# The tail of a decode block: w4 in five pieces instead of eight, the projection's row copied into spare bytes of w4's buffer, eight narrow last rows instead of six

## The chip, the cores and the metric

The kernel runs on one core of a Trainium2 chip. The metric is the device time of one execution in microseconds (us). Every run also has a span, from the first to the last profiled instruction of the core; the time is longer than the span by what lies outside it. Ratios are computed as the mean time of one kernel's runs over that of the other's of the same rounds, so they are not quite the ratio of the medians.

## The reference

One token goes through two branches that share the normalised input, and everything is summed. Cut to what matters:

```python
def reference(A_x, A_k_cache, A_v_cache, A_wq, A_wo, B_x, B_w1, B_w2, B_w3, B_w4):
    # A: 32 query heads, 4 key/value heads, 65536 cached keys of 128
    q = (x @ wq) ...                                   # 1024 -> 32 x 128
    p = softmax(q . k * 128 ** -0.5)
    o = p . v                                          # [cut]
    a = o @ wo                                         # 4096 -> 1024
    # B: a gated MLP for one position (w1, w2 act on a zero-padded shift), then
    h2 = gelu(layernorm(x1) @ w3) @ w4                 # 1024 -> 3584 -> 1024
    return x + a + (x1 + h2)
# bf16 data; caches 4 x 65536 x 128 each for k and v; w4 is 3584 x 1024
```

## The kernel before

One queue loads everything in a fixed order into three buffers of 64 KB a partition: wq, w3, w1 and w2, then the key and value blocks of 8 MB in turn, with wo before the last value block, and w4 last. A buffer is refilled when its last reader is done. What the change touches is the end of that stream. All products of one token are accumulated in one PSUM bank, psB (PSUM is where TensorE's sums stand until another engine copies them out): `row_acc(j, ...)` puts the j-th half of the output row into column group j of TensorE, so two matmuls run side by side. The last rows of w4 ("narrow") run as four quarters in four column groups in another pair of banks, into which the sum of everything else is added by a small fp32 matmul.

```python
W4_PIECES = (6, 5, 6, 4, 3, 2, 1, 1)     # rows (of 2 KB a partition) of each load of w4, 28 in all
NARROW = 6                               # last rows in four column groups
AHEAD = 3                                # of these, the ones before the sums
# [cut]
    def project(g):                      # o of head group g times its part of wo, 16 matmuls
        # [cut] groups 0..2 into tail["rows"][0:1, 0:2, :], group 3 by row_acc

    def add_projection():
        rows = ppool.tile([1, 2, 512], F32, name="o_rows", tag="p")   # tag "p": one buffer, shared with p_sb
        nc.vector.tensor_copy(out=rows[:], in_=tail["rows"][0:1, 0:2, :])
        for j in range(2):
            row_acc(j, ident_f[0:1, 0:1], rows[0:1, j, :])

    def compute_w4(lo, hi):              # row c of w4: two matmuls of 512 columns
        wt = st.tiles["w4"]
        for c in range(lo, hi):
            for j in range(2):
                row_acc(j, hT[:, c:c + 1], wt[:, D * c + 512 * j:D * c + 512 * (j + 1)])
# [cut]
    for g in range(HKV - 1):
        project(g)
    add_projection()
    compute_v(NU - 1)                    # last value block, its scaling, its gather (pe) and oT
    early = sum(W4_PIECES[:2])
    compute_w4(0, early)
    project(HKV - 1)
    compute_w4(early, FC - NARROW)
    sums = ogpool.tile([64, 512], F32, name="sums", tag="og")
    nc.scalar.copy(out=sums[:], in_=psB[0:64, :])
    # [cut] quarters: two PSUM banks; quarter_acc: four matmuls of 256 columns, one a column group
    narrow_rows(FC - NARROW, FC - NARROW + AHEAD, start=True)
    quarter_acc(...)                     # adds the sums, fp32
    narrow_rows(FC - NARROW + AHEAD, FC)
    # [cut] two casts, one store
```

`p_sb`, the probabilities, is read by the last value matmul. So the copy into `o_rows`, which shares its buffer, has to wait for it.

## Time and profile before

| | before |
|---|---|
| time, median of the first three runs | 401.93 us (400.98 to 401.99) |
| span of the profile | 399.0 us |
| loaded | 169.87 MB, 98.9% of the 16 load engines' time |
| TensorE busy, VectorE busy | 59%, 52% |

In the lines below PE is TensorE's matmuls, PEld its weight loads, DVE is VectorE, ACT ScalarE, POOL GpSimd, and an L with a number is a line of the kernel. "Half rate" means that the trace lists TensorE's granted clock as 0.50 of full. These are lines of the page of before: busy time of the engines, the busy share of the load engines in 40 slices, the packets, and the queues (q1 carries the loads, q8 fetches instructions).

```profile
span 399.0 us, 2590 instructions
...
PE 234.1 (59%) x1368; PEld 45.6 (11%) x874; DVE 209.4 (52%) x155; ACT 27.6 (7%) x36; POOL 5.3 (1%) x28
...
DMA  9998999999999999999999999999999999999996
...
DMA packets 4576, 170.03 MB, mean 426 GB/s; under 512 B 467, under 2 KB 469, under 8 KB 982
...
q1 hardware_dynamic: 4560, 169.87, 98.9%
q8 instruction: 9, 0.15, 0.2%
```

The load queue is full from end to end. The time is the time of 170 MB of loads, plus a start and a tail. The tail is read from the timeline (start, duration, engine, line, operation; in brackets the idle time ahead of it and what ended it):

```profile
384.41 1.21 DVE L459 COPY o_rows<-o_acc 1x1024 f32<-1x1024 f32 x1 [14.25 <-PE oacc L414]
...
385.68 1.05 PE L223 MATMUL psB<-o_rows,ident_f 1*32 1x512 f32 x4 [1.33 <-DVE o_rows L459]
...
388.53 0.80 PE L435 MATMUL pm_e<-ol,sel8big 128*128 128x129 f32 x2
...
392.88 2.11 PE L223 MATMUL psB<-big,hT 128*32 128x512 bf16 x18
...
395.46 0.58 ACT L486 COPY sums<-psB 64x512 f32<-64x512 f32 x1 [27.91 <-PE psB L223]
...
396.09 0.64 PE L493 MATMUL pm_r<-sums,ident_f 64*32 64x256 f32 x8 [0.35 <-ACT sums L486]
...
396.66 0.51 PE L493 MATMUL pm_r<-big,hT 128*32 128x256 bf16 x12
...
397.25 0.43 DVE L510 CAST out_t<-pm_r 64x256 bf16<-64x256 f32 x1 [6.91 <-PE pm_r L493]
```

The copy of the projection's row (L459) stood behind the last value matmul; TensorE then waited 1.33 us for it. The last line of L493 covers the last three rows of w4, twelve matmuls; the last four of them, for the last row, start at 396.89, while the trace has the last piece landed at 396.68. The chain that ended last says the same: it goes through TensorE (psB, pm_r), not through a load.

```profile
384.41 1.22 DVE o_rows L459
...
385.68 2.92 PE psB L223 x14
...
389.33 5.57 PE psB L223 x45
...
395.46 0.59 ACT sums L486
...
396.09 1.13 PE pm_r L493 x20
...
397.25 0.43 DVE out_t L510
```

### The profile page before, as it was taken

The numbers are of one execution on the slowest core, as the hardware profiler recorded it, in microseconds if no ns is written. First come the engines' busy times: TensorE is split into PE (matmuls) and PEld (weight loads), VectorE is DVE, ScalarE is ACT, GpSimd is POOL, SyncE is SP. The second block draws the span as 40 slices with busy tenths as digits, with TensorE's granted clock in tenths as the row PEclk, the third lists the DMA queues.
The fourth block names the chain that finished last, engine by engine and source line by source line (L and its number), as shares of the span: only waits on it lengthen the run. The fifth ranks groups of instructions, "written<-read, shape, count | busy, mean of one in ns | idle before, by whom it ended". The sixth has DMA issues, their size and how long they took to land.

```text
span 399.0 us, 2590 instructions
## 1 busy us (share of the span) xinstructions
PE 234.1 (59%) x1368; PEld 45.6 (11%) x874; DVE 209.4 (52%) x155; ACT 27.6 (7%) x36; POOL 5.3 (1%) x28
## 2 busy tenths in 40 slices
PE   0561960691569237733974296439443945494987
PEld 0210000000200110011001110101010002010133
DVE  0620010965196559634953795269449932884131
ACT  1001010003000200020002000200100020002000
POOL 2000000000000000000000000000000000000000
PEclk9996896696769787966695679569976886598799
DMA  9998999999999999999999999999999999999996
GB/s 421 420 454 372 437 453 473 434 420 420 422 428 420 440 466 435 420 427 427 435 420 440 447 447 420 422 420 447 427 442 440 440 420 394 425 450 447 393 420 255
DMA packets 4576, 170.03 MB, mean 426 GB/s; under 512 B 467, under 2 KB 469, under 8 KB 982
## 3 DMA queue, kind: packets, MB, share of 16 engines
q1 hardware_dynamic: 4560, 169.87, 98.9%
q8 instruction: 9, 0.15, 0.2%
q14 instruction: 1, 0.01, 0.0%
q10 hardware_dynamic: 6, 0.00, 0.0%
HBM read 169.87 MB, written 0.00 MB: 426 GB/s over the span
## 4 chain that ended last, share of the span: by engine, by line
DMA 48%; DVE 25%; PE 21%; ACT 3%; another core or an unknown queue 2%; issue 1%; DVEq 0%; ACTq 0%
DMA big<-in_A_k_cache_dram 42%; DVE big L359 19%; PE sc L364 8%; DMA big<-in_A_wq_dram 5%; PE oacc L414 5%; PE o_acc L453 3%; DVE mx L369 3%; ACT p_sb L382 3%; DVE p_sb L385 2%; PE psB L223 2%; PE psq L289 1%; DVE m L373 0%; PE pm_mx L371 0%; PE pm_mx L378 0%
## 5 line engine op out<-in xcount | busy, mean ns | idle before, releaser
L364 PE MATMUL sc<-big,qdiag 128*128 128x512 bf16 x512 | 130.2, 416 | 64.2 <-DVE big L359 63.9
L359 DVE STREAM_TRANSPOSE big<-big 128x4096 f32<-128x4096 f32 x32 | 139.4, 4413 | 50.7 <-DMA big<-in_A_k_cache_dram 50.7
L414 PE MATMUL oacc<-big,p_sb 128*32 128x512 bf16 x512 | 45.1, 522 | 34.5 <-DVE p_sb L385 34.5
L369 DVE TENSOR_REDUCE mx<-sc 128x1 f32<-128x2048 f32 x8 | 18.3, 2292 | 30.4 <-PE sc L364 30.4
L364 PEld LDWEIGHTS <-qdiag 128*128 128x128 bf16 x128 | 13.2, 103 | 176.7 <-issue 146.4
L382 ACT ACTIVATE p_sb<-sc,nball 128x2048 bf16<-128x2048 f32 x8 | 15.7, 1967 | 218.3 <-DVE nball L380 218.3
L385 DVE STREAM_TRANSPOSE p_sb<-p_sb 128x2048 bf16<-128x2048 bf16 x8 | 18.5, 2312 | 18.0 <-ACT p_sb L382 18.0
L414 PEld LDWEIGHTS <-p_sb 128*32 128x32 bf16 x512 | 16.8, 126 | 59.5 <-DVE p_sb L385 35.1
L289 PE MATMUL psh<-big,ln_rep_b 128*32 128x512 bf16 (+1 forms) x64 | 12.4, 941 | 8.6 <-DMA big<-in_B_w_dram 8.6
L453 PE MATMUL o_acc<-big,oT 128*1 128x512 bf16 x48 | 13.5, 453 | 2.4 <-ACT p_sb L382 2.4
L371 PE MATMUL pm_mx<-ident_f,mx 128*1 128x128 f32 x8 | 2.2, 270 | 19.1 <-DVE mx L369 19.1
L328 DVE STREAM_TRANSPOSE h_row<-h_row 128x896 bf16<-128x896 bf16 x1 | 1.1, 1111 | 21.7 <-ACT h_row L327 21.7
L423 DVE SCALAR_TENSOR_TENSOR og<-oacc,wb,og 128x512 f32<-128x512 f32 x4 | 3.0, 746 | 15.2 <-PE oacc L414 15.2
L459 DVE COPY o_rows<-o_acc 1x1024 f32<-1x1024 f32 x1 | 1.2, 1212 | 14.2 <-PE oacc L414 14.2
L237 PE MATMUL pm_ln<-ln_rowsum_a,ones_f 128*128 128x1 f32 x2 | 0.6, 347 | 12.6 <-DVE ln_rowsum_a L235 12.6
L435 PE MATMUL pm_e<-ol,sel8big 128*128 128x129 f32 x8 | 2.6, 414 | 7.9 <-DVE ol L434 7.9
L313 POOL COPY qdiag<-qx 32x32 bf16<-32x32 bf16 x16 | 3.2, 203 | 279.2 <-PE sc L364 250.5
L228 DVE STREAM_TRANSPOSE x_t<-x_row 32x256 bf16<-32x256 bf16 x4 | 2.5, 616 | 8.2 <-DMA x_row<-in_A_x_dram 8.1
L223 PE MATMUL psB<-big,hT 128*32 128x512 bf16 x44 | 6.5, 448 | 0.0
L289 PE MATMUL psq<-big,ln_rep_a 128*32 128x512 bf16 x64 | 5.2, 499 | 1.1 <-DMA big<-in_A_wq_dram 1.1
L378 PE MATMUL pm_mx<-ident_f,rep 1*128 1x1 f32 x8 | 1.9, 235 | 5.0 <-DVE rep L375 5.0
L420 ACT COPY og<-oacc 128x512 f32<-128x512 f32 x4 | 2.3, 585 | 34.3 <-PE oacc L414 34.3
(101 smaller groups left out, 75.1 us busy)
## 6 DMA issues: line engine op xcount, KB each, us to landing
big<-in_A_wo_dram SPq DMA_DIRECT2D x1, 8192.0 KB, 36.8
big<-in_B_w_dram SPq DMA_DIRECT2D x1, 7168.0 KB, 38.1
big<-in_B_w_dram SPq DMA_DIRECT2D x2, 2048.0 KB, 45.9
big<-in_B_w_dram SPq DMA_DIRECT2D x2, 1536.0 KB, 27.3
big<-in_B_w_dram SPq DMA_DIRECT2D x1, 1280.0 KB, 24.1
big<-in_B_w_dram SPq DMA_DIRECT2D x1, 1024.0 KB
big<-in_B_w_dram SPq DMA_DIRECT2D x1, 768.0 KB, 30.8
big<-in_B_w_dram SPq DMA_DIRECT2D x1, 512.0 KB, 31.6
```

The costliest lines, as they stand in the source:

```text
L223: nc.tensor.matmul(psB[32 * j:32 * j + 32, :], lhsT=lhsT.to_broadcast([lhsT.shape[0], 32]), rhs=rhs, start=start, stop=False, tile_positio ...
L289: nc.tensor.matmul(acc[32 * q:32 * q + 32, i, 0:n], lhsT=rep[:, c, :], rhs=cols(c, i, q), start=(c == 0), stop=(c == DC - 1), tile_positio ...
L313: nc.gpsimd.tensor_copy(out=qdiag[at, LEAD:].rearrange("p (x c) -> p x c", x=4)[:, :, 32 * a:32 * a + 8], in_=qx[at, :, 8 * g:8 * g + 8])
L359: nc.vector.transpose(out=words, in_=words)
L364: nc.tensor.matmul(sc[:, e, :], lhsT=qdiag[:, c0:c0 + P], rhs=cols[:, s, e, :, b2, :, r], start=(s == 0 and b2 == 0 and r == 0), stop=(s = ...
L369: nc.vector.reduce_max(out=mx[:], in_=sc[:].rearrange("p e n -> p (e n)"), axis=AX.X)
L382: nc.scalar.activation(out=p_sb[:], in_=sc[:], func=ACTF.Exp, bias=nball[:, b:b + 1], scale=SCALE, accum_out=group["lall"][:, b:b + 1])
L385: nc.vector.transpose(out=flat, in_=flat)
L414: nc.tensor.matmul(oacc[32 * q:32 * (q + 1), :], lhsT=pT[:, e, 32 * t:32 * (t + 1)], rhs=vt[:, :, e, t, :], start=(e == 0 and t < 4), stop ...
L423: nc.vector.scalar_tensor_tensor(out=og[:], in0=oacc[:], scalar=wb[:, 1:2], in1=og[:], op0=ALU.mult, op1=ALU.add)
L435: nc.tensor.matmul(pe[:, 0:DH + 1], lhsT=sel8big[:], rhs=ol[:], start=True, stop=True)
L453: nc.tensor.matmul(tail["rows"][0:1, h2, :], lhsT=oT[g][:, j:j + 1], rhs=wt[:, g, j, 512 * h2:512 * (h2 + 1)], start=(g == 0 and j == 0), ...
```

## The change

Its intent: make the end of TensorE's work depend on the last load alone. The w4 loads become fewer and are cut so that a piece of 12 rows may come late and the last piece is still one row. The projection's row is copied, as soon as it is summed, into bytes of w4's own buffer that no w4 load writes, so it no longer waits for the probabilities' buffer. Eight rows instead of six go through the narrow path and five of them ahead of the sums, so that the sums are taken two rows earlier. `issue_after` fixes the order of TensorE's instructions without a wait.

```diff
-W4_PIECES = (6, 5, 6, 4, 3, 2, 1, 1)
-NARROW = 6
-AHEAD = 3
+W4_PIECES = (8, 12, 5, 2, 1)
+FIRST = 3
+AT_ONCE = 1
+NARROW = 8
+AHEAD = 5
 # [cut: row_acc, compute_v, group_rows and project return their matmul]
-    def add_projection():
-        rows = ppool.tile([1, 2, 512], F32, name="o_rows", tag="p")
-        nc.vector.tensor_copy(out=rows[:], in_=tail["rows"][0:1, 0:2, :])
+    def copy_projection():
+        tail["o"] = st.tiles["w4"][0:1, FC * D:FC * D + 2 * D].bitcast(F32)
+        nc.vector.tensor_copy(out=tail["o"].rearrange("p (j n) -> p j n", j=2), in_=tail["rows"][0:1, 0:2, :])
+
+    def add_projection():
         for j in range(2):
-            row_acc(j, ident_f[0:1, 0:1], rows[0:1, j, :])
+            row_acc(j, ident_f[0:1, 0:1], tail["o"][:, 512 * j:512 * (j + 1)])
 # [cut]
-    add_projection()
-    compute_v(NU - 1)
-    early = sum(W4_PIECES[:2])
-    compute_w4(0, early)
-    project(HKV - 1)
-    compute_w4(early, FC - NARROW)
+    copy_projection()
+    summed = compute_v(NU - 1)
+    with tc.issue_after(summed):
+        add_projection()
+    early = sum(W4_PIECES[:AT_ONCE])
+    compute_w4(0, FIRST)
+    with tc.issue_after(tail["gathered"]):
+        compute_w4(FIRST, early)
+    projected = project(HKV - 1)
+    with tc.issue_after(projected):
+        compute_w4(early, FC - NARROW)
```

More of the change, by code (lines that the diff above doesn't have):

```diff
@@ L222, in row_acc @@
     def row_acc(j, lhsT, rhs, start=False):
-        nc.tensor.matmul(psB[32 * j:32 * j + 32, :], lhsT=lhsT.to_broadcast([lhsT.shape[0], 32]), rhs=rhs, start=start,
-                         stop=False, tile_position=(0, 32 * j), skip_group_check=True)
+        return nc.tensor.matmul(psB[32 * j:32 * j + 32, :], lhsT=lhsT.to_broadcast([lhsT.shape[0], 32]), rhs=rhs, start=start,
+                                stop=False, tile_position=(0, 32 * j), skip_group_check=True)
     x_t = ppool.tile([P, DC, 32], BF16, name="x_t", tag="p")
@@ L413, in compute_v @@
                 q = t % 4
-                nc.tensor.matmul(oacc[32 * q:32 * (q + 1), :], lhsT=pT[:, e, 32 * t:32 * (t + 1)],
-                                 rhs=vt[:, :, e, t, :], start=(e == 0 and t < 4),
-                                 stop=(e == SUBS - 1 and t >= 12), tile_position=(0, 32 * q))
+                mm = nc.tensor.matmul(oacc[32 * q:32 * (q + 1), :], lhsT=pT[:, e, 32 * t:32 * (t + 1)],
+                                      rhs=vt[:, :, e, t, :], start=(e == 0 and t < 4),
+                                      stop=(e == SUBS - 1 and t >= 12), tile_position=(0, 32 * q))
         st.done(("V", u))
@@ L425, in compute_v @@
         group_rows(g, og, ol)
+        return mm.ins
     oT = {}
@@ L434, in group_rows @@
         nc.vector.tensor_reduce(out=ol[:, 0:DH], in_=og[:].rearrange("p (s d) -> p d s", d=DH), axis=AX.X, op=ALU.add)
-        nc.tensor.matmul(pe[:, 0:DH + 1], lhsT=sel8big[:], rhs=ol[:], start=True, stop=True)
+        tail["gathered"] = nc.tensor.matmul(pe[:, 0:DH + 1], lhsT=sel8big[:], rhs=ol[:], start=True, stop=True).ins
         msk = small.tile([P, 16, 8], F32, name="msk", tag="msk")
@@ L450, in project @@
                 if g == HKV - 1:
-                    row_acc(h2, oT[g][:, j:j + 1], wt[:, g, j, 512 * h2:512 * (h2 + 1)])
+                    mm = row_acc(h2, oT[g][:, j:j + 1], wt[:, g, j, 512 * h2:512 * (h2 + 1)])
                     continue
@@ L455, in project @@
                                  stop=(g == HKV - 2 and j == 7), tile_position=(0, 0))
+        return mm.ins if g == HKV - 1 else None
+    def copy_projection():
+        tail["o"] = st.tiles["w4"][0:1, FC * D:FC * D + 2 * D].bitcast(F32)
+        nc.vector.tensor_copy(out=tail["o"].rearrange("p (j n) -> p j n", j=2), in_=tail["rows"][0:1, 0:2, :])
     def add_projection():
-        rows = ppool.tile([1, 2, 512], F32, name="o_rows", tag="p")
-        nc.vector.tensor_copy(out=rows[:], in_=tail["rows"][0:1, 0:2, :])
         for j in range(2):
-            row_acc(j, ident_f[0:1, 0:1], rows[0:1, j, :])
+            row_acc(j, ident_f[0:1, 0:1], tail["o"][:, 512 * j:512 * (j + 1)])
     def compute_w4(lo, hi):
```

## The prediction

> What bounds the kernel now. The span is 399.0 us; the load queue carries 169.87 MB in packets that fill 98.9% of 16 engines' time (page, part 3), and no slice of DMA is below 8 tenths except the last (part 2). TensorE is busy 59%, VectorE 52%. It is a stream of loads with a tail, and the change touches only the tail, behind the last value block, which lands at 379.27.
>
> The tail, from the timeline and the landings. The 28 rows of w4 follow without a hole: 11 rows have landed at 386.05, 17 at 389.73, 24 at 394.12, 26 at 395.38, 27 at 396.04, all at 396.68: 0.62 us a row, whatever the piece. TensorE runs almost without a hole from 379.9 and is a little late: the wide rows end at 395.4, the copy of the sums takes 0.58, their fp32 matmuls start at 396.09, and only at 396.66 the last three rows go, 0.11 us each. The last row starts at 396.89, 0.2 us after it landed, and ends at 397.17; the casts end at 397.68, the span at 399.0. The chain of waits names TensorE (psB, pm_r) here, but landing and chain end within 0.2 us of each other.
>
> What the change does.
> 1. The projection's row no longer waits for the probabilities' buffer. In before its copy stood behind the last value matmul (VectorE idle 14.2 us, copy 384.41 to 385.62, TensorE idle 1.3 us) and pushed the output scaling back by 1.1 us. After, it is copied near 381, and its fp32 rows follow the value matmuls at about 384.4.
> 2. The gather comes about 1.1 us sooner (near 387.0), the last projection near 389. Holding w4 rows behind the gather can leave TensorE idle 0.9 us; harmless.
> 3. Pieces of 8, 12, 5, 2, 1: estimated landings 384.2, 391.6, 394.7, 396.0, 396.6 (0.62 us a row). The 12-row piece comes late for TensorE, but its 24 matmuls in two column groups take 12 x 0.215 = 2.6 us, to 394.3. The copy of the sums starts there, hidden behind the five narrow rows ahead (5 x 0.11). The sums' matmuls end near 395.8. The last row then waits for its landing alone.
> 4. Three fewer DMAs: a packet of 2 KB takes 0.085 us, one of 4 KB 0.165, so a packet costs some 0.005 us beside its bytes; about 0.1 us of stream in all. Bytes are unchanged.
>
> On the critical path: 0.2 us of TensorE lateness and up to 0.1 us of stream. The 1.3 us hole and VectorE's 1.1 us mostly become slack before the last landing. Gain 0.2 to 0.35 us, under 0.1%, below the run-to-run spread of before (400.98 to 401.99).
>
> Predicted: 401.6 us, 8 in 10 within 400.7 to 402.3. Faster by over 2%: 0.01; within 2%: 0.98; slower: 0.01.
>
> What would show it: last landing within 0.3 us of before; the row's copy before 383; TensorE idle before the last row until its landing; last matmul ending 0.3 us after it instead of 0.5; landing to end of span 2.1 us instead of 2.3.
>
> What would make it wrong: the copy into w4's tile ordered behind w4's loads (then some 10 us lost). TensorE's clock is 0.50 from 387.1 to 390.3 in before; the Trainium skill (TensorE: Matmul & The Clock Gate, Part 1) ties half rate to recent idleness in free-running windows. Half rate over the 24 matmuls at 391.6 would end them near 396.8 and cost up to 2 us.

## The result

| | before | changed |
|---|---|---|
| time, six runs each of the same rounds | 401.26 us median (400.97 to 401.99) | 400.68 us median (400.60 to 400.81) |
| ratio of the runs | | 0.9982 (95%: 0.9969 to 0.9995) |
| span of the profile | 399.0 | 398.7 |
| last w4 landing | 396.68 | 396.50 |

The predicted 401.6 us with its range of 400.7 to 402.3 missed the measured 400.68 us, and the forecast gain of 0.2 to 0.35 us stands against 0.7 us between the means of these runs (0.0018 x 401).

The same lines of the page after the change:

```profile
span 398.7 us, 2595 instructions
...
PE 229.6 (58%) x1372; PEld 44.2 (11%) x878; DVE 209.4 (53%) x155; ACT 27.6 (7%) x36; POOL 5.3 (1%) x28
...
DMA packets 4144, 170.03 MB, mean 427 GB/s; under 512 B 419, under 2 KB 421, under 8 KB 678
...
q1 hardware_dynamic: 4128, 169.87, 98.9%
q8 instruction: 9, 0.15, 0.2%
```

The bytes are the same. There are 432 packets fewer, and TensorE is 4.5 us less busy in this profile, which is not on the way to the end. The tail of the changed kernel:

```profile
380.70 1.21 DVE L463 COPY big<-o_acc 1x1024 f32<-1x1024 f32 x1 [10.50 <-PE o_acc L456]
...
384.05 1.05 PE L225 MATMUL psB<-big,ident_f 1*32 1x512 f32 x4
...
386.76 0.49 PE L438 MATMUL pm_e<-ol,sel8big 128*128 128x129 f32 x2 [0.92 <-DVE ol L437]
...
391.54 2.77 PE L225 MATMUL psB<-big,hT 128*32 128x512 bf16 x24 [1.31 <-DMA big<-in_B_w_dram]
...
394.34 0.58 ACT L497 COPY sums<-psB 64x512 f32<-64x512 f32 x1 [26.75 <-PE psB L225]
...
395.31 0.64 PE L504 MATMUL pm_r<-sums,ident_f 64*32 64x256 f32 x8
...
396.54 0.29 PE L504 MATMUL pm_r<-big,hT 128*32 128x256 bf16 x4 [0.24 <-DMA big<-in_B_w_dram]
...
396.90 0.43 DVE L521 CAST out_t<-pm_r 64x256 bf16<-64x256 f32 x1 [8.63 <-PE pm_r L504]
```

The row's copy (L463) ends at 381.9, and its fp32 matmuls follow the value matmuls at 384.05. The gather (L438) comes 1.8 us sooner than in this profile of before, in which TensorE ran at half rate just then, and 0.6 us sooner than in a second profile of before (b_again, at 387.39). The twelve wide rows wait for the 12-row piece until 391.54, and the last four matmuls wait for the last landing (396.50) and start at 396.54. The chain that ended last is now a load, to the end but for one row, one cast and the store:

```profile
363.39 33.10 DMA big<-in_B_w_dram
396.50 0.04 issue
396.54 0.34 PE pm_r L504 x4
```

So nearly every landmark of the prediction is there (only the last projection, at 388.3 instead of 389, is off by more than 0.4 us): landings forecast at 384.2, 391.6, 394.7 and 396.6 came at 384.19, 391.50, 394.60 and 396.50; the copy is before 383; the last matmul ends 0.33 us after the last landing. Landing to end of span is 2.2 us (2.1 forecast, 2.3 before). What failed is the time, and this is what the experiments were about.

### The profile page after: what moved, and what is told of

Same layout as the page of the kernel before. It is cut to its first block, busy times and chain, and to the rows that moved or that the text cites. A ratio compares the mean times of both kernels' runs of the same rounds, so it can differ in the third digit from the quotient of the medians.

```text
span 398.7 us, 2595 instructions
## 1 busy us (share of the span) xinstructions
PE 229.6 (58%) x1372; PEld 44.2 (11%) x878; DVE 209.4 (53%) x155; ACT 27.6 (7%) x36; POOL 5.3 (1%) x28
## 4 chain that ended last, share of the span: by engine, by line
DMA 56%; DVE 21%; PE 17%; ACT 2%; another core or an unknown queue 2%; issue 1%; SPq 0%; DVEq 0%; ACTq 0%
DMA big<-in_A_k_cache_dram 42%; DVE big L361 15%; PE sc L366 11%; DMA big<-in_B_w_dram 8%; DMA big<-in_A_wq_dram 5%; PE oacc L416 4%; DVE p_sb L387 2%; DVE mx L371 2%; ACT p_sb L384 2%; PE psq L291 1%; SPq L187 0%; PE pm_mx L373 0%; DVE m L375 0%; PE pm_mx L380 0%
## 5 line engine op out<-in xcount | busy, mean ns | idle before, releaser
L416 PE MATMUL oacc<-big,p_sb 128*32 128x512 bf16 x512 | 43.0, 502 | 34.5 <-DVE p_sb L387 34.5
L438 PE MATMUL pm_e<-ol,sel8big 128*128 128x129 f32 x8 | 2.3, 370 | 8.8 <-DVE ol L437 8.8
L463 DVE COPY big<-o_acc 1x1024 f32<-1x1024 f32 x1 | 1.2, 1211 | 10.5 <-PE o_acc L456 10.5
L225 PE MATMUL psB<-big,hT 128*32 128x512 bf16 x40 | 4.8, 380 | 1.3 <-DMA big<-in_B_w_dram 1.3
```

Of the source, the lines that this page charges most:

```text
L225: return nc.tensor.matmul(psB[32 * j:32 * j + 32, :], lhsT=lhsT.to_broadcast([lhsT.shape[0], 32]), rhs=rhs, start=start, stop=False, tile_ ...
L416: mm = nc.tensor.matmul(oacc[32 * q:32 * (q + 1), :], lhsT=pT[:, e, 32 * t:32 * (t + 1)], rhs=vt[:, :, e, t, :], start=(e == 0 and t < 4), ...
```

## The experiments

Sixteen experiments were run (some of them one of the two kernels once more), in four sets of four, each set on its own chip with eleven runs of before. "Time outside" below is a run's time minus its span; a "stray" is a run with over 2.15 us outside, where most have 2.0. First the runs of before of all four sets, since they carry the argument: their medians were 401.06, 400.94, 400.94 and 400.95 us.

### Set 1: is TensorE or the load stream what ends before?

The theory to start with, A, was that TensorE is late in before and that half-rate stretches of its clock make runs long; the rival, B, that the load stream does.

**b_again**: before, unchanged (no edit).

> The kernel before, unchanged, to see where its spread comes from. Theory A (TensorE is the last to finish in the tail, so a half-rate stretch of its clock there lengthens the run): runs spread over 0.5 us or more, 400.9 to 402; the profile, if it falls on a slow run, shows longer half-rate stretches between 384 and 396 than the 3.4 us seen before, and the last w4 landing still at 396.7. Rival B (the load stream itself varies or is slowed by the many small pieces): the last landing moves with the run's time. Mean 401.3 either way.

Measured: median 400.96 us (400.82 to 401.83, five runs), ratio 1.0001 (0.9989 to 1.0013). The profile is of the run of 401.83 us, and its span is 398.9, no longer than others. The tail of this profile of before:

```profile
394.62 0.58 ACT L486 COPY sums<-psB 64x512 f32<-64x512 f32 x1 [27.04 <-PE psB L223]
395.44 0.29 PE L493 MATMUL pm_r<-big,hT 128*32 128x256 bf16 x4 [0.64 <-DMA big<-in_B_w_dram]
...
395.66 0.64 PE L493 MATMUL pm_r<-sums,ident_f 64*32 64x256 f32 x8
...
396.23 0.81 PE L493 MATMUL pm_r<-big,hT 128*32 128x256 bf16 x12
396.74 0.10 PEld L493 LDWEIGHTS <-hT 128*32 128x32 bf16 x3 [0.30 <-issue]
```

There is no half-rate stretch between 372 and the end of the span here, the sums are copied 0.84 us sooner than in the first profile, and the last four matmuls start at 396.74, 0.04 us after the last landing (396.70). So before, too, can end on the last load; the 0.2 us of lateness were of the first profile, in which TensorE ran at half rate from 387.1 to 390.5. That the half rate made them fits b_pad40 below, which has the same stretch and the same late copy of the sums (395.47). But it depends on where the stretch falls: b_pad8 below has one from 386.2 to 389.6, and its last row starts 0.04 us after its landing. And the 1 us that this run took longer than the others is neither in the tail nor in the stream: it lies outside the span (2.93 us; most runs have 2.0). Both theories missed that.

**b_warm**: six useless matmuls in the hole behind the value matmuls, so that TensorE does not pause there. The main part of the edit:

```diff
+    with tc.issue_after(last):
+        for i in range(DUMMIES):   # 6
+            last = nc.tensor.matmul(tail["rows"][:, 2 + i % 2, :], lhsT=qdiag[:, 0:P],
+                                    rhs=st.tiles["wo"][:, 512 * i:512 * (i + 1)], start=True, stop=True).ins
 # [cut: issue_after keeps the order of the matmuls behind it]
```

> Before with six useless 128x512 matmuls (about 1.3 us) in the hole in which TensorE waits for the projection row's copy; all other orders kept. Theory A with the clock as cause: no half-rate stretch between 387 and 390, TensorE some 1.5 us earlier at the wide rows, the last row waits for its landing; time 0.3 to 0.7 us under before and little spread (0.3 us), as the changed kernel. If the hole itself and not the clock matters, the time stays that of before or rises by up to 0.1 us. Rival B: no change.

Measured: median 400.95 us (400.88 to 401.10), ratio 0.9994 (0.9981 to 1.0007); no half-rate stretch in its tail. But b_again had none either, so the test does not tell the clock from chance. Nor does it decide on a gain of 0.3 us: the means differ by 0.2 us, and the interval reaches from a loss of 0.3 to a gain of 0.8 us.

**b_late3** and **a_late3**: three useless matmuls (0.65 us) ahead of the last wide row, in before and in the changed kernel.

```diff
-    compute_w4(early, FC - NARROW)
+    wide = compute_w4(early, FC - NARROW - 1)
+    with tc.issue_after(wide):
+        for i in range(LATE):   # 3
+            wide = nc.tensor.matmul(tail["rows"][:, 2 + i % 2, :], lhsT=qdiag[:, 0:P],
+                                    rhs=st.tiles["wo"][:, 512 * i:512 * (i + 1)], start=True, stop=True).ins
+    with tc.issue_after(wide):
+        compute_w4(FC - NARROW - 1, FC - NARROW)
```

> Before with three useless 128x512 matmuls (0.65 us at full clock) ahead of its last wide row. Theory A (no slack in TensorE's tail): 0.5 to 0.65 us slower than before. Rival B (the landing decides): no change beyond 0.1 us.

> The changed kernel with the same three useless matmuls ahead of its last wide row. Theory A (the change gave TensorE slack in front of the last landing, 0.5 us or more): 400.7 us, within 0.1 us of the changed kernel, the last row still waits for its landing. If the gain were only earlier work and no slack: 0.4 to 0.65 us slower, 401.1 to 401.3.

Measured: b_late3 401.29 us median (400.80 to 402.60, six runs), ratio 1.001 (0.9996 to 1.0023); a_late3 400.86 us (400.71 to 400.95, five runs), ratio 0.9992 (0.998 to 1.0004). From the timeline of b_late3, the copy of the sums and the weight load of the last row, which landed at 396.63:

```profile
394.54 0.58 ACT L494 COPY sums<-psB 64x512 f32<-64x512 f32 x1 [26.83 <-PE psB L224]
...
396.67 0.10 PEld L501 LDWEIGHTS <-hT 128*32 128x32 bf16 x3 [0.30 <-issue]
```

In this profile before swallowed the delay whole, so theory A, that TensorE has no slack there, fell as a general statement. In two of the six runs the span was 399.5 and 399.6, though (no profile fell on them), and four of the six were strays (2.23 to 3.10 us outside). The changed kernel kept its spans at 398.7 to 399.0 with the same burden, and had no strays (1.95 to 2.11). Its tail (the copy of the sums, then the last three rows in one go, the last of them landed at 396.45):

```profile
395.17 0.58 ACT L505 COPY sums<-psB 64x512 f32<-64x512 f32 x1 [27.60 <-PE psB L226]
...
396.36 0.51 PE L512 MATMUL pm_r<-big,hT 128*32 128x256 bf16 x12
```

The last row starts at 396.59, 0.14 us after its landing: the expectation that it would still wait failed in this profile. The burden used up the changed kernel's slack and a little more.

### Set 2: pieces, and the end of the instruction stream

The traces hold one more thing that moves: nine fetches of 16 KB by q8. The Trainium skill (Runtime: NRT & Kernel Launch, Instruction fetch mechanics) says that an engine's instructions are refilled in blocks of 16 KiB, 256 instructions. The traces agree: nine packets of 16384 bytes, in before 182 to 320 of TensorE's recorded instructions apart (262 on average); 248 instructions more (a_pad247 below) make ten of them, 48 fewer (a_minus48) make eight. In the programs with nine, the ninth starts when TensorE has begun 2220 to 2270 recorded instructions. Before has 2262, the changed kernel 2270. So the ninth fetch falls at the very end. These are the stretches behind the tail in the first profile of before and in b_again, with the share and rate of the load engines as the last two columns; past the end of the span a fetch is all that is left to see (16 KB in 1.5 us are 11 GB/s):

```profile
core 0: us, PE busy (x) PEld busy (x) DVE busy (x) ACT busy (x) POOL busy (x), PEclk, DMA share, GB/s
398.00:399.00 1.00, 0.00 (x0) 0.00 (x0) 0.00 (x0) 0.00 (x0) 0.00 (x0) 1.00 0.08 18
401.00:402.50 1.50, 0.00 (x0) 0.00 (x0) 0.00 (x0) 0.00 (x0) 0.00 (x0) 0.92 0.00 0
```

```profile
398.00:399.00 1.00, 0.00 (x0) 0.00 (x0) 0.00 (x0) 0.00 (x0) 0.00 (x0) 1.00 0.01 2
401.00:402.50 1.50, 0.00 (x0) 0.00 (x0) 0.00 (x0) 0.00 (x0) 0.00 (x0) 0.65 0.04 11
```

The packet records give the starts: 398.17 us in the first, 401.13 us in b_again, the run with 1 us more outside the span. (The first profile's span is 399.0, while 398.8 is listed for the run of 400.82 us, so I can't say which time goes with this profile, though one of the texts below takes it to be 400.82.) In the changed kernel's first profile it is 396.07, at the moment when the last load packet ends (396.08).

**b_pad40**: before with 40 one-column matmuls (41 instructions) early, behind the q projection, where TensorE has holes.

```diff
     compute_wq()
+    filler = ps_M.tile([P, 512], F32, name="pm_pad", tag="pm")
+    for i in range(40):
+        nc.tensor.matmul(filler[0:32, 0:1], lhsT=xn_rep[:, 0, :], rhs=xn_rep[:, 0, 0:1], start=True, stop=True)
     compute_w3()
```

> Before with 41 more TensorE instructions (40 matmuls of one column) early, where TensorE has holes. In the two profiles of before, the last 16 KB instruction fetch starts at 398.17 (run of 400.82) and at 401.13 (run of 401.83, with the same span of 398.9), behind TensorE's last instruction; in the changed kernel it starts at 396.07, before the end. Theory C (before's stray runs, over 2.5 us of time outside the span, come from where the program's end falls against an instruction fetch): with 41 more instructions the last fetch starts before 396, all runs have time minus span of 2.0 to 2.2, none above 401.3, mean 401.0. Rival D (the stray runs are chance, or come from the tail's lateness): 2 in 10 runs still have 2.5 or more. The last landing stays at 396.7 in both.

Measured: 402.30 us median (401.03 to 402.43), ratio 1.0028 (1.0016 to 1.004), time outside 1.99 to 2.11 in all five. The fetch moved as expected, to 395.72. What was not expected: four of five runs had spans of 400.3 or 400.4 us instead of 398.9 and took 402.3 to 402.4 us; in the profile, of one of these, the last landing came at 398.13 instead of 396.7, though the last value block landed as in before (379.27). The completion packets (4 bytes, one for each engine and load) in the packet records end so:

```
before    396.08  396.14  396.21  396.24
b_pad40   396.04  396.15  396.23  397.68
```

The skill (DMA: Bandwidth & Descriptors, Why a DMA increments its semaphore by 16 and not by 1) says that each of up to 16 engines posts its own completion, and only all 16 tell of the landing. Here 15 came in time, and one 1.45 us behind. A fetch takes 0.92 to 1.36 us in these traces. That the fetch held the engine that was late is inferred, since the trace does not name engines.

**a_pad247**: the changed kernel with 248 more instructions of the same kind, which brings its end to where before's lies between two fetches.

```diff
+    for i in range(247):   # [cut: the rest as in b_pad40]
```

> The changed kernel with 248 more TensorE instructions early, which puts its end where before's end lies against the 256-instruction fetches (2518 against 2262). Theory C: last fetch behind the last instruction, about a third of the runs with time minus span of 2.5 or more; mean 400.9 to 401.1. Rival D: as the changed kernel, 400.6 to 400.9, all differences 2.0 to 2.2. The last landing stays at 396.5 in both.

Measured: 402.62 us median (401.87 to 403.49), ratio 1.0044 (1.0032 to 1.0056). One run of five had 2.99 us outside, the one of 403.49, and one 2.27; the profile is of the first and has the last fetch at 402.79. But all spans are longer (399.9 to 400.8). In the profile two things are late. The 12-row piece landed at 392.58 instead of 391.5; one more fetch than in the changed kernel lies inside the stream (35.73), but that it is the cause is not shown. And TensorE ran at half rate from 393.8 to 397.2, over the wide rows. The microsecond from 395 on in the changed kernel's first profile, then here with the next one (the granted clock is the third column from the right):

```profile
395.00:396.00 1.00, 1.00 (x28) 0.38 (x20) 0.00 (x0) 0.00 (x0) 0.00 (x0) 1.00 0.44 168
```

```profile
395.00:396.00 1.00, 1.00 (x12) 0.52 (x10) 0.00 (x0) 0.00 (x0) 0.00 (x0) 0.50 0.40 156
396.00:397.00 1.00, 1.00 (x19) 0.54 (x12) 0.00 (x0) 0.10 (x1) 0.00 (x0) 0.50 0.08 31
```

The sums were copied at 396.89 instead of 394.34, and the last row started at 398.35, 0.77 us after its landing (397.57): TensorE, not a load, ended this run. This is the danger that the prediction named, half rate over the 24 wide matmuls. The experiment mixed these things and tells of theory C only that one run.

**a_oldpieces** and **b_pieces**: the pieces alone, undone in the changed kernel and done in before.

```diff
-W4_PIECES = (8, 12, 5, 2, 1)
+W4_PIECES = (6, 5, 6, 4, 3, 2, 1, 1)
```

> The changed kernel with the eight pieces of before (6, 5, 6, 4, 3, 2, 1, 1). Theory E (fewer pieces end the load stream sooner): last landing back at 396.68, span 398.9, time 400.85 to 400.95, 0.2 us over the changed kernel. If the pieces' number does not matter: 396.5 and 400.7.

```diff
-W4_PIECES = (6, 5, 6, 4, 3, 2, 1, 1)
+W4_PIECES = (8, 12, 5, 2, 1)
-    early = sum(W4_PIECES[:2])
+    early = sum(W4_PIECES[:1])
```

> Before with the five pieces of the changed kernel and nothing else (six narrow rows, row copied behind the value matmuls). Theory E: last landing 396.5; the wide rows 20 and 21 wait for the 5-row piece (394.6), so the sums' matmuls come near 395.8 to 396.4 and the last row ends within 0.2 us of where it ends in the changed kernel; span 398.7 to 398.9, 400.7 to 400.9 at best, with more spread than the changed kernel since TensorE has less slack.

Measured: a_oldpieces 402.01 us median (400.63 to 402.49, six runs), ratio 1.0022 (1.001 to 1.0035); b_pieces 401.07 us (400.82 to 401.38), ratio 1.0003 (0.9991 to 1.0015). b_pieces confirms theory E for the landing (396.47 against 396.68 to 396.70 in three profiles of before). a_oldpieces seems to overshoot it (396.82 instead of the expected 396.68), and a_oldpieces2 below to refute it (396.52, eight pieces and as early as the changed kernel). But the stream ahead of w4 differs by some 0.4 us from profile to profile; counted from the landing of the last value block, the last landing comes 17.40, 17.40 and 17.39 us later in before, 17.39 in both of the changed kernel with eight pieces, and 17.20, 17.19 and 17.21 us later in the changed kernel, 17.19 in b_pieces. So five pieces save 0.20 us of stream, in either kernel. b_pieces also shows that this is not enough: with six narrow rows TensorE starts the last row at 396.7, 0.2 us late, and the time does not move. That the eight narrow rows, five of them ahead, are what makes the changed kernel gain from the landing is inferred; they were not tried alone. a_oldpieces lost much more than the 0.2 us expected: three spans of 399.4 or 399.5, and four runs with 2.65 to 2.99 us outside. That was a new question.

### Set 3: the changed kernel again, and the fetch

> The changed kernel unchanged, on one chip with its variants and before. If the forecast gain was right and only its base (401.93, the median of three runs) was off: 0.25 to 0.4 us under before, whose median has been 400.94 and 401.06 in 22 runs since; so 400.6 to 400.75, time minus span 2.0 to 2.1 in every run. If the gain is really 0.7 us: before near 401.3, this 400.6.

**a_again**, the changed kernel unchanged: 400.87 us median (400.73 to 401.61, six runs), before 400.94 (400.76 to 402.10, eleven runs), ratio 0.9995 (0.9983 to 1.0007). That is 0.07 us between the medians and 0.2 us between the means, under the expected 0.25 to 0.4, and the median lies above the expected 400.75. Nor is before near 401.3: only two of its runs are far above, with more than 3 us outside. Time outside in the changed kernel: 2.00 to 2.13 in all six. One run had a span of 399.6.

**a_oldpieces2**, the same edit as a_oldpieces.

> The changed kernel with before's eight pieces once more, for the profile of another run: four of six runs took 402.0 to 402.5, with spans of 399.0 to 399.5 and time minus span of 2.7 to 3.0. Theory F (a 16 KB instruction fetch that starts before the last load packet holds one load engine for its 1.1 us): the span of a long run comes with a fetch before 396.4 and one completion packet about 1 us behind the others. Theory C2 (a fetch behind the end of the span lengthens the time outside it by its own 1 us): time minus span near 3.0 comes with a fetch after 399. If neither is seen in a slow profile, both fall for this kernel.

Measured: 401.29 us median (400.95 to 402.10, six runs), ratio 1.0007 (0.9994 to 1.002). The profile is of a stray, 401.96 us with a span of 398.7, so 3.26 outside. Theory C2 said what it should show, and it does:

```profile
398.00:399.00 1.00, 0.00 (x0) 0.00 (x0) 0.00 (x0) 0.00 (x0) 0.00 (x0) 0.50 0.01 2
401.00:402.50 1.50, 0.00 (x0) 0.00 (x0) 0.00 (x0) 0.00 (x0) 0.00 (x0) 0.60 0.05 11
```

The fetch starts at 401.07. Together with b_again and a_pad247 that makes three profiles with a last fetch behind 400, and these are the three with about 3 us outside; no other profile whose time is known has more than 2.3. (b_late3's profile has eight fetches on record and 2.23 outside; whether a ninth came after the record's end can't be seen.) That the late fetch makes the time outside, and is not itself late because something else held the end up, these three do not show. The long spans of this kernel were not caught in a profile. What decides whether a kernel with the very same number of instructions fetches before or after its end is open.

**a_pad40**: the filler of b_pad40 in the changed kernel.

> The changed kernel with 41 more TensorE instructions early, so that the last instruction fetch starts about 41 instructions sooner, near 395, inside the load stream, as it did in before with the same filler (395.72, last landing 398.13). Theory F: last landing near 397.6, 401.7 to 402.1, time minus span 2.0 to 2.1. If the filler itself costs (1.3 us early in the kernel) and not the fetch: landing of the last value block later than 379.3 by as much as the end.

Measured: 402.09 us median (401.89 to 402.39, six runs), ratio 1.0024 (1.0012 to 1.0036); time outside 1.98 to 2.09. The fetch starts at 395.07, the value block landed when it always does (379.36), and the last piece is late. The chain that ended last:

```profile
363.56 34.31 DMA big<-in_B_w_dram
397.87 0.04 issue
397.91 0.34 PE pm_r L507 x4
```

The landing is at 397.87 instead of 396.50; the last two completion packets come at 396.59 and 397.44, the others by 395.95. So what theory F foretold came in both kernels. In this profile, though, TensorE also ran at half rate over the wide rows (391.6 to 395.0) and was ready for the last row only 0.2 us before it landed (it is idle from 397.67); the late landing is shown, its share of the 1.2 us is not. And in a_again a fetch at 395.72 did no harm (landing 396.57), while in a_late3, with one at 395.95, the last landing is 17.32 us behind the value block, 0.12 more than in the changed kernel: it may depend on which engine the fetch meets, and that cannot be seen in the trace.

**b_pad8**: before with 8 instructions more, 2270 in all, as the changed kernel has.

```diff
+    for i in range(7):   # [cut: the rest as in b_pad40]
```

> Before with 8 more TensorE instructions early (2270, the changed kernel's number): the last fetch should start with the last row, near 396.5, behind the last load packet (396.25) and before the end. Theory C2: time minus span 2.0 to 2.2 in every run, median 400.9 to 401.0; no gain in the landing (396.7). If the fetch falls just before the last packet in some runs (theory F), those have spans of 399.5 or more.

Measured: 401.09 us median (400.95 to 401.76, six runs), ratio 1.0 (0.9988 to 1.0012). The fetch starts at 396.68 in the profile, as expected, but one run had 2.86 us outside and one 2.23. So the mere number of instructions does not set the strays.

### Set 4: the base, and no ninth fetch

> The changed kernel once more. If the forecast's gain was right and its base wrong: median 0.2 to 0.35 us under that of before and b_again2, 400.6 to 400.8, span 398.6 to 398.8 except for a rare run with a fetch on a load engine still at work. If the gain is 0.7 us: before at 401.3 or more.

> Before once more, for its base and one more profile: median 400.9 to 401.1, not 401.9; one or two runs in ten with time minus span of 2.6 or more; if the profile is of one of those, its last fetch comes after 400, else by 398.5.

**a_again2** and **b_again2**, both unchanged: 400.76 us median (400.58 to 400.87, six runs), ratio 0.9989 (0.9977 to 1.0001), and 400.93 us (400.88 to 401.15, six runs), ratio 0.9995; before in the same rounds 400.95 (400.89 to 402.53). Between the medians that is the forecast gain of 0.2 us, on a base of 400.95; between the means it is 0.4 us, since four of the eleven runs of before were strays. No run of b_again2 was a stray.

**a_minus48** and **b_minus48**: without the projections of two of the four groups, 48 TensorE instructions fewer. Their outputs are wrong, which doesn't matter for the times.

```diff
-    for g in range(HKV - 1):
+    for g in range(HKV - 2, HKV - 1):
         project(g)
 # [cut: the first matmul of the remaining group starts the sum]
```

> The changed kernel without the projections of the first two groups (a wrong result on purpose), 48 TensorE instructions fewer. If the ninth fetch makes the strays: no fetch between 385 and the end of the span, last landing 396.5, spans 398.6 to 398.8 in every run; time minus span 2.0 in every run if the end needs no fetch at all, near 3.0 in every run if it needs it behind the span. If the fetch has nothing to do with it: 1 run in 10 with a gap of 2.5 or more or a span over 399.2, as before.

> Before without the same projections (a wrong result on purpose): the same as for the changed kernel as to the fetch and the time outside the span. Last landing 396.7; spans 398.8 to 399.2, the longer ones with half-rate stretches of TensorE's clock behind 385.

Measured: a_minus48 400.77 us median (400.61 to 401.93), b_minus48 401.51 us (400.82 to 402.38), six runs each; ratios 0.9994 (0.998 to 1.0009) and 1.0013 (0.9994 to 1.0031). The ninth fetch is gone from the profile of a_minus48 (and from that of b_minus48):

```profile
q8 instruction: 8, 0.13, 0.1%
```

The time outside is 1.95 to 2.05 in all twelve runs. Before has over 2.15 in 15 of its 55 runs of sets 1 to 4, eight of them over 2.5. So the strays outside the span hang on the ninth fetch at the end: move it well ahead of the end or take it away, and they are gone (none in 11 runs of the two fillers of 41, none in 12 here). How it lengthens the time is not shown. But the spans are not cured: three of b_minus48 are 400.1 to 400.4 and one of a_minus48 is 399.9. No profile fell on one of these, so their cause is open; the half rate over the wide rows of a_pad247 is one candidate.

## Why the prediction was right or wrong

**The step that failed is the last one, the subtraction: "Predicted: 401.6 us, 8 in 10 within 400.7 to 402.3".** It set a gain of 0.3 us against a base of 401.93, the median of three runs. In the 55 runs of before in sets 1 to 4 the median is 400.96 and the mean 401.10. Two of the three first runs lay 1 us above that. Two checks were at hand and not made. The three runs were themselves 400.98, 401.99 and 401.93, so a median of them could be anything in a spread of 1 us. And the trace gave a span, of which the reckoning said it would shrink to about 398.7. In most runs since (40 of the 55 of before, all 18 of the changed kernel) the time is the span plus 1.95 to 2.15 us, and 398.7 plus 2.0 is 400.7. The range, 400.7 to 402.3, was laid around the wrong centre and cut off exactly where the truth lies.

**The gain of 0.2 to 0.35 us was about right in size, with its terms mis-sized; that the sum came out is luck in part.** Over all 18 runs of the changed kernel (its six, a_again, a_again2) against the 55 of before, the mean time is 400.80 against 401.10 (0.30 us), the median 400.73 against 400.96 (0.23 us), the mean span 398.76 against 398.93 (0.18 us). Pooled over chips this is no paired result, but it lies between the pairs of a_again and a_again2 (ratios 0.9995 and 0.9989, so 0.2 and 0.4 us). The 0.7 us of the first pair contains two long runs of before (401.93 and 401.99) among its six. Term by term:

- *"Up to 0.1 us of stream"*: it was 0.20, from the last value block's landing to the last landing (17.40, 17.40, 17.39 us in three profiles of before, 17.20, 17.19, 17.21 in three of the changed kernel). The landings themselves, 396.68, 396.70, 396.70 against 396.50, 396.57, 396.57, differ by 0.15 on average. With 27 packets an engine fewer that is about 7 ns a packet (an estimate) and not 5. The trace of before has 0.0845 and 0.161 us as the medians of its 2 KB and 4 KB packets, which makes 8 ns; the prediction's 0.165 was too high. And the completion packets (9 ns each, three an engine fewer) had been left out.
- *"0.2 us of TensorE lateness"*: it was in one profile of three. In b_again and b_again2 the last row starts 0.04 us after its landing. I took one execution's half-rate stretch (387.1 to 390.5) for the kernel's state. The Trainium skill (TensorE: Matmul & The Clock Gate, Part 1) calls the windows free-running; the traces agree in that the half-rate stretches are 3.41 to 17.07 us long in steps of 3.41, and do not lie at the same times in all profiles of one kernel; that idleness brings them on was not tested. On average the span gained little or nothing from this: 0.18 us in all, which the landing alone accounts for.
- *Time outside the span*: it was not in the sum at all. It is 2.17 us on average in the 55 runs of before and 2.05 in the 18 of the changed kernel, in which none is over 2.15. That is the remaining 0.12 us of the 0.30. The changed kernel has its ninth instruction fetch at 395.7 to 396.4 in its three profiles, ahead of the end, but a_oldpieces and b_pad8, with as many instructions, stray too. Why the changed kernel does not is open.

**What was right.** The order of events in the tail, all landings to 0.1 us, the copy before 383, the hole before the gather that cost nothing, the wait for the landing at the end, and that the 1.3 us hole and 1.1 us of VectorE's work would be slack and no gain: the hole is still there in b_again (383.60 to 384.93), and the last row waits for its landing all the same. Of the two dangers named, the first did not come: the copy was not ordered behind the loads. The second, half rate over the wide rows, is in none of the changed kernel's three profiles, and its spans stayed within 398.5 and 399.0 in 17 of 18 runs, also in a_again2, whose profile has a half-rate stretch from 387.15 to 390.56, ahead of these rows. But it is real: it came in the profiles of a_pad247 and a_pad40, and in the first the last row started 0.77 us late.

What stays open: which engine a fetch meets, what sets its time when the program ends near a fetch, and the long spans of b_minus48, b_late3, a_oldpieces, one run of a_minus48 and one of a_again. The row's copy in its own bytes and the eight narrow rows were not tried alone.

## What to carry to other kernels

Build a forecast time from the span that the trace shows plus the constant that lies outside it, and take a base of three runs that differ by 1 us for what it is. When a kernel is one long stream of loads, a saved hole in the tail is worth only what the last landing allows; look for what the landing itself waits for, here the number of packets and, it seems, an instruction fetch in the last 2 us of the stream. Compare landings between profiles from a common event shortly before, not from the start of the span: here that turned 0.15 us, with a counterexample (a_oldpieces2), into 0.20 us in both kernels. When a profile shows an instruction fetch near the program's end, runs may stray; shifting it can cost more than it saves: with 41 useless early instructions the runs took 1.0 to 1.4 us longer.

## What the Trainium skill lacked or had wrong

- Runtime: NRT & Kernel Launch, Instruction fetch mechanics, calls the cost of crossing a 16 KiB block mostly hidden. In a kernel bound by loads it seems not always to be: with a fetch at 395.07 or 395.72, inside the last 2 us of the stream, the last landing came 1.4 us late in the profiles of a_pad40 and b_pad40, and the medians rose by 1.2 and 1.4 us over those of the kernels they were made from, in the same rounds. In a_again a fetch at 395.72 cost nothing that shows, and that the fetch held the late engine is inferred.
- The same page says nothing of a block boundary at the program's end: with the last fetch behind 400 us the time outside the span was 2.9 to 3.3 us instead of 2.0 (three profiles), and with 48 instructions fewer and no ninth fetch 1.95 to 2.05 in twelve runs. That the fetch is the cause of the time, and not only its companion, is not shown.
- DMA: Bandwidth & Descriptors, Why small descriptors are slow, tells of a fixed overhead a packet and holds joining descriptors to be worth it at 256 B or less. Here w4's loads in packets of 2 to 24 KB instead of 2 to 12, 27 packets an engine fewer, brought the last landing 0.20 us closer to the last value block's, about 7 ns a packet (an estimate). That was most of the gain of 0.23 to 0.30 us.
